# Loads of the second block in another order, and x's adding transfer moved to the seventh unit

## The chip, the cores and the metric

The kernel runs on one core of one Trainium2 chip. The metric is the device time of one launch in microseconds (us), the median of three runs. Profiles are of one execution each.

## What is computed

A decayed scan (an attention of the state-space kind, in chunks) is followed by a gated feed-forward layer. The reference, cut to what matters:

```python
def _attn_ref(x, a, B, C):                      # x: 4 x 8 x 768 x 32, B and C: 4 x 8 x 768 x 16
    log_a = np.log(np.clip(a, 1e-06, 1.0))
    for c in range(nc):                          # chunks of 32 steps
        cum = np.cumsum(la, axis=-1)
        L = np.exp(cum[:, :, :, None] - cum[:, :, None, :]) * causal
        M = np.einsum('bhin,bhjn->bhij', Cc, Bc) * L
        y_intra = np.einsum('bhij,bhjd->bhid', M, xc)
        y_inter = np.einsum('bhin,bhnd->bhid', Cc, state) * np.exp(cum)[:, :, :, None]
        y[:, :, sl] = y_intra + y_inter
        state = decay_full[:, :, None, None] * state + np.sum(Bx, axis=2)

def _moe_ref(x, w_gate, w_val, w_out):           # x: 3072 x 256, d_ff 1536
    g = x @ w_gate
    silu = g * (1.0 / (1.0 + np.exp(-g)))
    return (silu * (x @ w_val)) @ w_out
```

## The kernel before

**Tiling.** The 768 steps are cut into six blocks of 128 steps (k = 0 to 5; the text calls k = 1 the second block), each of two pieces of 64. One block holds 512 tokens (4 batches by 128 steps). Per block the scan part makes decays (`L` between steps, `E` for the carried state), scores `S`, the mixed matrix in `L`, states `T` and the output `y`; then the feed-forward part runs over 12 units of 128 hidden columns: `gate_val` (two PSUM banks, the tiles `gv`), `silu` on ACT, `product` on DVE (both write `sg`), a split of the product into a high and a low part (`hh`), and `project` into `po`.

**Two kinds of feed-forward matmul.** For the first block the first nine units (`WHOLE = 9`) multiply plain 32-bit floats: the weights `wg0w` to `wg8w` and x in `xf`. All others multiply high and low parts: weights `wg..h` and `wg..l`, x in `xh` and `xl`. So the first block's units 9, 10 and 11 are the first that read its `xh` and `xl`.

**Where the parts come from.** Each weight piece arrives as 64-bit integers' words (`wg9r`, loaded by `w_fetch`) and is turned into floats by a chain over engines: `w_magnitude` and `w_rest` on ACT, `w_range` on POOL for most pieces, `w_shift`, `w_sign` and `w_round` on DVE; then `w_high` on ACT. The low part of the first nine pieces is made by ACT writing the negative of the weight (`w_minus`) and POOL issuing a transfer that adds the weight to it (`w_low`, `accum_op=ALU.add`). x of the first block goes the same way: `first_high` and `first_minus` on ACT, twice each, and `first_low`, one adding transfer of 512 KB issued by POOL:

```python
    def first_low():
        ge.dma_start(xl[0], whole[0], accum_op=ALU.add)
```

Weight pieces 9 to 11 need no transfer: DVE subtracts (`w_low`).

**The second block's loads** are `bc` (B and C, 512 KB), `L` (the decays, each row sent to 64 partitions, two transfers of 520 KB), `xb` (x and B, 768 KB) and `E` (260 KB), all on SP's queue, which also issues the weight pieces. `heads_apart` (`Cz`) reads `bc`, `scan_j` reads `L`, `weigh_b` reads `xb`, `scan_n` reads `E`, all on DVE here.

**What sets the order.** Every step is an `Op` with an engine, a cost, a rank, what it needs and a `lag` that stands for the transfer behind an issue. `Plan.order` plays these through and issues the steps in the order that it finds; `plan.follow` adds needs "issued after" for the lists in `ORDER`. Each engine then runs its instructions in that order. A step with `lag` occupies a modelled bus, so a changed lag can move steps on every engine. All engine instructions have line 191, that of the recording helper; the tile names tell them apart.

Of the kernel before, what the change touches and what calls it, by code (L numbers as in the profile page):

```python
# [19 lines left out]
P = 128  # L20
# [24 lines left out]
class Plan:  # L45
# [19 lines left out]
    def add(self, engine, cost, run, rank, needs=(), takes=(), uses=(), gives=None, kind=None, lag=0.0, rows=1.0, slack=0.0):  # L65
        engines = [(engine, cost)] if cost is not None else engine
        self.ops.append(Op(engines, run, rank, needs, takes, uses, gives, kind, lag, rows, slack, cost is None))
# [134 lines left out]
def scan_moe_kernel(ctx: ExitStack, tc, aj, an, bc, xb, wgv, wo, cst, own, out):  # L202
    nc = tc.nc
    PSUM = bass.MemoryType.PSUM
    te, ve, se, ge, sp = (
        Ordered(tc, e) for e in (nc.tensor, nc.vector, nc.scalar, nc.gpsimd, nc.sync)
    )

    def pool(name, bufs, stack=ctx, **kw):
        return stack.enter_context(tc.tile_pool(name=name, bufs=bufs, **kw))  # L210
# [5 lines left out]
    raw = pool("raw", RAW)  # L216
# [14 lines left out]
    clipped = dram.tile([2, P, NA * W], F32, name="clipped")  # L231
# [79 lines left out]
    def first(b, i):  # L311
        return b < BATCH and not i
# [189 lines left out]
    xh, xl = {}, {}  # L502
# [170 lines left out]
    rest = {}  # L673
# [29 lines left out]
    def do(f, *a):  # L703
        return lambda *e: f(*a, *e)
# [6 lines left out]
    add = plan.add  # L711
# [10 lines left out]
    def due(k, f=0):  # L722

        return begin[k] + f * (GV if k else PACE0)

    def at(n):

        return divmod(n, NF)

    def due_sum(k, f):  # L730
        return begin_sum[k] + f * PO
# [12 lines left out]
    for i in range(NW):  # L744
        r = due(0, i) - 1.0 if i < NF else due_sum(0, 2 * (i - NF)) - 1.0
        if i < NF:
            add("SP", 0.48, do(w_fetch, i), r - 9.0, takes=[("raw", ("raw", i))], gives=("raw", i), lag=1.3)
        else:
            add("Act", 0.1, do(w_fetch, i, se), due(*at(LAST[i - NF])) + 2, [("si", *at(LAST[i - NF]))], takes=[("raw", ("raw", i))], gives=("raw", i), lag=1.3)
        add("Act", 0.57, do(w_magnitude, i, "Act"), r - 5.5, [("raw", i)], takes=[("sg" if i < NF else "w", ("w", i))], gives=("mag", i))  # L750
        far = i in FAR
        e, c = ("Pool", 2.2) if far else ("DVE", 0.335)
        add(e, c, do(w_range, i, ge if far else ve), r - 4.5, [("mag", i), *([("round", i - 1)] if i == 1 else [])], gives=("range", i))
        add("Act", 0.57, do(w_rest, i, "Act"), r - 4.5, [("raw", i), *([("xf", 3)] if i == 3 else [])], gives=("rest", i))
        add("DVE", 0.335, do(w_shift, i), r - 4.2, [("range", i)], gives=("shift", i))
        add("DVE", 0.6, do(w_sign, i), r - 3.9, [("shift", i)], gives=("sign", i))
        add("DVE", 0.6, do(w_round, i), r - 3.3, [("sign", i), ("rest", i)], uses=[("raw", i)], gives=("round", i))
        if i < WHOLE:
            r = due(1, i) - LATER
        add("Act", 0.57, do(w_high, i, "Act"), r - 2.7, [("round", i), ("gv", 0, 0, 0)], gives=("wh", i))  # L760
        whole_done = [("gv", 0, i, m) for m in range(2)]
        if i < WHOLE:
            add("Act", 0.57, do(w_minus, i), r - 2.6, [("round", i), ("gv", *at(MINUS[i]), 0)], gives=("minus", i))
            add("Pool", 1.2, do(w_low, i), r - 2.5, [("wh", i), ("minus", i), *whole_done], uses=[("w", i)], gives=("wl", i), lag=3.0)
        else:
            add("DVE", 0.6, do(w_low, i), r - 1.5, [("wh", i)], uses=[("w", i)], gives=("wl", i))


    add("-", 0.0, lambda: None, -7.9, gives="all", lag=0.9)
    add("Pool", 1.0, clip_all, -9, ["all"], gives="clipped")  # L770
    add("SP", 0.48, do(write_all, sp, slice(0, FEW)), -9, ["clipped"], gives="few", lag=1.5)
    add("Act", 0.1, do(write_all, se, slice(FEW, P)), -1.6, ["clipped", ("rest", 0)], gives="written", lag=1.5)


    for k in range(NB):
        r = due(k)
        SLACK = min(k / 2, 1.0)
        z = -5 if not k else r + LEAD[min(k, 3)]
        L, E, BC, XB, CZ, TT = ("L", k), ("E", k), ("bc", k), ("xb", k), ("Cz", k), ("T", k)
        add("-", 0.0, do(new_decays, k) if k else lambda: None, z - 12, [("decays", k - 1)] if k else [], takes=[("L", L), ("E", E)], gives=("decays", k))  # L780
        late = [("raw", LATE[k])] if k in LATE else []
# [12 lines left out]
        if not k:  # L794
            add("-", 0.0, lambda: None, -9, takes=[("xl", "rows")], gives="rows", lag=0.2)
            for i in range(3):
                add("DVE", 0.35, do(clip_rows, i), (-9, -8.9, -5)[i], ["rows", *([("scan0", 1)] if i == 2 else [])], gives=("clip", i))
            for b in range(BATCH + 1):
                r = z + 0.5 + b if b < BATCH else -1.3
                for i in range(2 if b < BATCH else 1):  # L800
                    t = ("spread", b, i)
                    add("PE", 0.25 if first(b, i) else 0.45, do(spread, b, i), r + 0.5 * i, [("clip", b % 2 if b < BATCH else 2), "pick"], takes=[("mm" if first(b, i) else "at", t)], uses=[t, "rows"], gives=t, kind="s")
                    need = [t, ("decays", 0)] + ([("scan0", b)] if i else [])
                    done = ("E", 0) if b == BATCH else ("L", 0, b) if i else ("scan0", b)
                    add("DVE", 0.63, do(scan_spread, b, i), r + 0.5 * i, need, uses=[t], gives=done)
        else:
            add("SP", 0.96, do(load_aj, k), FETCH["aj"] if k == 1 else z - 12, ["few", "written", ("decays", k), *late], gives=("aj", k), lag=4.3)
            add("SP", 0.48, do(load_an, k), FETCH["an"] if k == 1 else z - 9, ["few", "written", ("decays", k), *late], gives=("an", k), lag=2.4)
            for b in range(BATCH):
                add("DVE", 1.14, do(scan_j, k, b), z + 0.5 + b, [("aj", k)], gives=("L", k, b), slack=1.0)  # L810
            add("DVE", 1.17, do(scan_n, k), z + 6, [("an", k)], gives=("E", k), slack=1.0)
# [26 lines left out]
        uses = [L, E, XB, BC, *y, TT]  # L838
# [16 lines left out]
        if not k:  # L855
            add("-", 0.0, new_whole, -9, [("clip", 2)], takes=[("xl", "xf")], gives="xf")
            add("-", 0.0, do(new_x, 0), due(0, WHOLE) - 9, [("xf", i) for i in range(2 * K)], takes=[("xh", ("xh", 0)), ("xl", ("xl", 0))], gives=("x", 0))
            for g in range(2):
                r = due(0, WHOLE) - 7 + 2 * g
                add("Act", 0.57, do(first_high, g, "Act"), r, [("x", 0)], gives=("xh", 0, g))  # L860
                add("Act", 0.57, do(first_minus, g), r + 0.5, [("x", 0)], gives=("minus", "x", g))
            add("Pool", 1.2, first_low, due(0, WHOLE) - 4.5, [("minus", "x", g) for g in range(2)], uses=["xf"], gives=("xl", 0, 0), lag=3.0)
            for i in range(2 * K):
                add([("Act", 0.36)], None, do(x_whole, i), -1 + i / 10, [("vals", i) if i < 2 else ("y", 0), "xf"], uses=[y[i]], gives=("xf", i))
            continue
# [6 lines left out]
    for k in range(NB):  # L872
        xs = [(t, k, i) for t in ("xh", "xl") for i in range(2 * K if k else 2) if k or t == "xh" or not i]
        for f in range(NF):
            r = due(k, f)
            need = [*xs, ("wh", f), ("wl", f)]
            c = 1.4
            x = [("xh", k), ("xl", k)]
            if not k and f < WHOLE:
                need = [("round", f), *(("xf", i) for i in range(2 * K))]  # L880
                c = 1.72
                x = ["xf"]
            gv = [("gv", k, f, m) for m in range(2)]
# [5 lines left out]
            r = due_sum(k, f) - 4  # L889
# [4 lines left out]
        for n, (m, t, fs) in enumerate(sums_of(k)):  # L894
# [4 lines left out]
            r = due_sum(k, fs[0]) + n * 0.01  # L899
# [25 lines left out]
FETCH = dict(aj=10.0, an=35.0, bc=12.0, xb=31.0)  # L925
LATER = 3.0
WHOLE = 9
LAST = (5, 6, 9, 10, 11, 12)
MINUS = (3, 3, 4, 5, 9, 9, 10, 10, 11)
FEW = 8  # L930
# [1 line left out]
PAGE = 4.4  # L932
ORDER = (
    ["few", ("raw", 2)],
    [("raw", 8), ("bc", 1), ("aj", 1), ("raw", 9), ("xb", 1), ("raw", 10), ("an", 1), ("raw", 11)],
    [("xf", 3), ("mag", 2), ("rest", 2), ("mag", 3)],
    [("y", 0), ("xf", 2)],
)
LEAD = {1: -30.0, 2: -44.0, 3: -44.0}
LATE = {}  # L940
# [49 lines left out]
```

## Time and profile before

| | |
|---|---|
| median of 3 runs | 353.0 us |
| the runs | 351.2, 353.0, 353.35 us |
| the profiled execution's own time | 353.25 us |
| its span, first to last instruction | 351.4 us |
| instructions | 7415 |
| TensorE clock granted, mean | 0.998 |
| bytes moved by DMA | 30.98 MB, mean 88 GB/s |

The profiled execution's own time is 1.85 us above its span. The page gives each engine's busy time and then the span in 40 slices of 8.8 us; the views behind it (the timeline of one engine, the chain that ended last, sums over windows, the list of DMA issues) are in microseconds from the span's start. A bracket in a timeline row tells how long the engine was idle ahead of it and what ended that.

### The profile page before, as it was taken

The page shows a single profiled execution, that of the slowest core. Times are in us where ns is not written, and L with a number is a line of the kernel's source. Part 1 is how long each engine was busy: PE and PEld are TensorE (multiplying, and loading weights), DVE is VectorE, ACT ScalarE, POOL GpSimd, SP SyncE. Part 2 cuts the span into 40 slices and gives each one's busy share as a digit, 9 for nine tenths or more (in the row PEclk, how much of TensorE's full clock was granted, in tenths as well). Part 3 has the DMA queues.
Part 4 walks back from the last instruction along what each step waited for, and adds up shares of the span by engine and source line. Part 5 has one row for each costly group of instructions (what it writes and reads, how often), then busy time and mean ns, then how long its engine had stood idle before and what let it go on. Part 6 is the DMA issues. An engine that isn't in the chain of part 4 may idle for free.

```text
span 351.4 us, 7415 instructions
## 1 busy us (share of the span) xinstructions
PE 341.9 (97%) x3195; PEld 267.2 (76%) x3196; DVE 232.1 (66%) x418; ACT 121.8 (35%) x222; POOL 45.3 (13%) x36
## 2 busy tenths in 40 slices
PE   7999988999999999999999999999999999999996
PEld 5644436888878888888888888888888888888895
DVE  6996999999888856676447677447666440465220
ACT  3785766643445422212322222231212230222221
POOL 2395563522012000000000000000000000000000
PEclk9999999999999999999999999999999999999999
DMA  7999972994000671000382000281100000100001
GB/s 262 289 316 246 259 162 69 247 249 130 0 2 2 185 179 60 0 2 3 105 184 76 0 2 2 74 211 39 41 3 2 2 2 0 60 2 0 0 2 60
DMA packets 9935, 30.98 MB, mean 88 GB/s; under 512 B 1287, under 2 KB 2055, under 8 KB 9263
## 3 DMA queue, kind: packets, MB, share of 16 engines
q1 hardware_dynamic: 7168, 24.23, 23.6%
q0 software_dynamic: 1440, 2.88, 4.7%
q10 hardware_dynamic: 1295, 3.40, 3.2%
q8 instruction: 25, 0.41, 0.5%
q14 instruction: 7, 0.06, 0.1%
HBM read 24.28 MB, written 3.35 MB: 79 GB/s over the span
## 4 chain that ended last, share of the span: by engine, by line
PE 83%; DMA 6%; DVE 5%; issue 1%; ACT 1%; ACTq 0%; DVEq 0%; SPq 0%
PE gv L191 49%; PE po L191 28%; DMA wg10r<-in_wgv 6%; PE y L191 4%; PE S L191 1%; DVE wg8w L191 1%; DVE sg L191 1%; DVE wg2w L191 1%; DVE wg9w L191 0%; DVE wg1w L191 0%; DVE wg0w L191 0%; DVE L L191 0%; DVE E L191 0%; DVE wg10w L191 0%; DVE T L191 0%
## 5 line engine op out<-in xcount | busy, mean ns | idle before, releaser
L191 DVE TENSOR_TENSOR sg<-gv,sg 128x512 f32<-128x512 f32 x72 | 49.5, 687 | 65.4 <-PE gv L191 65.2
L191 ACT ACTIVATE sg<-gv 128x512 f32<-128x512 f32 x72 | 43.0, 597 | 105.5 <-PE gv L191 105.5
L191 DVE TENSOR_TENSOR hh<-sg,hh 128x512 fp32r<-128x512 f32 x72 | 49.3, 690 | 12.5 <-ACT hh L191 11.0
L191 ACT CAST hh<-sg 128x512 fp32r<-128x512 f32 x34 | 21.2, 623 | 30.1 <-PE po L191 17.7
L191 DVE TENSOR_TENSOR_SCAN L<-L,dj 128x520 f32<-128x520 f32 x20 | 24.6, 1248 | 10.2 <-DMA L<-clipped 10.2
L191 ACT COPY ob<-po 128x512 f32<-128x512 f32 (+1 forms) x13 | 7.2, 555 | 48.7 <-PE po L191 48.2
L191 DVE CAST hh<-sg 128x512 fp32r<-128x512 f32 x38 | 16.5, 434 | 2.4 <-PE po L191 1.2
L191 PE MATMUL po<-hh,wo0h 128*128 128x512 f32 (+1 forms) x52 | 15.3, 377 | 0.0
L191 PE MATMUL po<-hh,wo3h 128*128 128x512 f32 (+1 forms) x52 | 15.2, 375 | 0.0
L191 PE MATMUL po<-hh,wo1h 128*128 128x512 f32 (+1 forms) x52 | 15.2, 375 | 0.0
L191 PE MATMUL po<-hh,wo4h 128*128 128x512 f32 (+1 forms) x52 | 15.1, 373 | 0.0
L191 DVE TENSOR_TENSOR L<-S,L 128x512 f32<-128x512 f32 x24 | 15.1, 681 | 0.0
L191 PE MATMUL po<-hh,wo5h 128*128 128x512 f32 (+1 forms) x52 | 15.1, 373 | 0.0
L191 PE MATMUL po<-hh,wo2h 128*128 128x512 f32 (+1 forms) x52 | 15.0, 373 | 0.0
L191 PE MATMUL y<-L,xb 64*32 64x64 f32 x768 | 11.5, 239 | 0.0
L191 PEld LDWEIGHTS po<-hh,wo0h 128*128 128x128 f32 x52 | 9.5, 188 | 2.2 <-DVE hh L191 0.3
L191 PEld LDWEIGHTS y<-L,xb 64*32 64x32 f32 x768 | 9.5, 112 | 2.0 <-issue 1.8
L191 PEld LDWEIGHTS po<-hh,wo4h 128*128 128x128 f32 x52 | 9.5, 188 | 1.7
L191 PEld LDWEIGHTS po<-hh,wo5h 128*128 128x128 f32 x52 | 9.5, 188 | 1.7
L191 PEld LDWEIGHTS po<-hh,wo2h 128*128 128x128 f32 x52 | 9.5, 188 | 1.7
L191 PEld LDWEIGHTS po<-hh,wo1h 128*128 128x128 f32 x52 | 9.4, 188 | 1.8
L191 PEld LDWEIGHTS po<-hh,wo3h 128*128 128x128 f32 x52 | 9.4, 188 | 1.7
(298 smaller groups left out, 754.0 us busy)
## 6 DMA issues: line engine op xcount, KB each, us to landing
L<-clipped SPq DMA_DIRECT2D x10, 520.0 KB, 17.0
xb<-in_xb SPq DMA_DIRECT2D x6, 768.0 KB, 10.5
bc<-in_bc SPq DMA_DIRECT2D x6, 512.0 KB
out<-ob SPq DMA_DIRECT2D x11, 256.0 KB, 2.0
E<-clipped SPq DMA_DIRECT2D x5, 260.0 KB
wg0r<-in_wgv SPq DMA_DIRECT2D x1, 512.0 KB
wg1r<-in_wgv SPq DMA_DIRECT2D x1, 512.0 KB
wg2r<-in_wgv SPq DMA_DIRECT2D x1, 512.0 KB
```

What stands on the lines that cost most here:

```text
L191: ins = getattr(self.engine, name)(*a, **k)
```

## The change

Two kinds of lines change. The first are four `lag` values of the plan and the lists of `ORDER`: the second block's loads go `bc`, `aj` (which loads `L`), `xb`, `an` (which loads `E`) as before, but each of the last three now follows one weight piece more; a new list says that `Cz` of the second block is issued after `round` of piece 6. The second is one need: `first_minus` now waits for ("gv", 0, 6, 0), the first gate matmul of the seventh unit, so that the negative of x is written later, and with it the adding transfer `first_low` comes later.

```diff
-            add("Pool", 1.2, do(w_low, i), r - 2.5, [...], uses=[("w", i)], gives=("wl", i), lag=3.0)
+            add("Pool", 1.2, do(w_low, i), r - 2.5, [...], uses=[("w", i)], gives=("wl", i), lag=1.6)
...
-    add("SP", 0.48, do(write_all, sp, slice(0, FEW)), -9, ["clipped"], gives="few", lag=1.5)
-    add("Act", 0.1, do(write_all, se, slice(FEW, P)), -1.6, ["clipped", ("rest", 0)], gives="written", lag=1.5)
+    add("SP", 0.48, do(write_all, sp, slice(0, FEW)), -9, ["clipped"], gives="few", lag=2.6)
+    add("Act", 0.1, do(write_all, se, slice(FEW, P)), -1.6, ["clipped", ("rest", 0)], gives="written", lag=0.3)
...
-            add("SP", 0.96, do(load_aj, k), ..., gives=("aj", k), lag=4.3)
-            add("SP", 0.48, do(load_an, k), ..., gives=("an", k), lag=2.4)
+            add("SP", 0.96, do(load_aj, k), ..., gives=("aj", k), lag=4.8)
+            add("SP", 0.48, do(load_an, k), ..., gives=("an", k), lag=1.8)
...
-                add("Act", 0.57, do(first_minus, g), r + 0.5, [("x", 0)], gives=("minus", "x", g))
-            add("Pool", 1.2, first_low, ..., uses=["xf"], gives=("xl", 0, 0), lag=3.0)
+                add("Act", 0.57, do(first_minus, g), r + 0.5, [("x", 0), ("gv", 0, 6, 0)], gives=("minus", "x", g))
+            add("Pool", 1.2, first_low, ..., uses=["xf"], gives=("xl", 0, 0), lag=1.6)
...
-    [("raw", 8), ("bc", 1), ("aj", 1), ("raw", 9), ("xb", 1), ("raw", 10), ("an", 1), ("raw", 11)],
+    [("raw", 8), ("bc", 1), ("raw", 9), ("aj", 1), ("raw", 10), ("xb", 1), ("raw", 11), ("an", 1)],
...
+    [("round", 6), ("Cz", 1)],
```

Up to the issue of `wg8r` SP's row is the same, and so are POOL's and ACT's up to the eighth range and the third silu. SP's row from there (`in_wgv` is the weights' input; minus is before, plus is now):

```order
 L191 DMA wg8r<-in_wgv 128x1024
-L191 DMA bc_424<-in_bc 128x1024
+L191 DMA bc_421<-in_bc 128x1024
+L191 DMA wg9r<-in_wgv 128x1024
 L191 DMA L_372<-clipped 64x2080 x2
-L191 DMA wg9r<-in_wgv 128x1024
-L191 DMA xb_443<-in_xb 128x1536
 L191 DMA wg10r<-in_wgv 128x1024
+L191 DMA xb_446<-in_xb 128x1536
+L191 DMA wg11r<-in_wgv 128x1024
 L191 DMA E_373<-clipped 128x1x520
-L191 DMA wg11r<-in_wgv 128x1024
```

Weight pieces 9, 10 and 11 each moved ahead of one load of the second block: `L`, `xb` and `E`.

DVE's row after the range of piece 5 came in, before (a TENSOR_SCALAR on `wg..w` is a shift, a SCALAR_TENSOR_TENSOR on `wg..w` a sign, an ISA a rounding, a TENSOR_TENSOR on `sg` a product, a SCALAR_TENSOR_TENSOR on `L` a scan):

```order
L191 TENSOR_SCALAR wg5w<-wg5w 128x512
L191 TENSOR_SCALAR Cz_463<-bc_424,cs 128x4x128 x2
L191 SCALAR_TENSOR_TENSOR wg5w<-wg5r,wg5w 128x512
L191 TENSOR_TENSOR sg_2_461<-gv_2_1_457,sg_2_461 128x512
L191 ISA wg5w<-wg5r,wg5w 128x1024
L191 TENSOR_SCALAR wg6w<-wg6w 128x512
L191 SCALAR_TENSOR_TENSOR wg6w<-wg6r,wg6w 128x512
L191 TENSOR_SCALAR wg7w<-wg7w 128x512
L191 ISA wg6w<-wg6r,wg6w 128x1024
L191 SCALAR_TENSOR_TENSOR wg7w<-wg7r,wg7w 128x512
L191 TENSOR_TENSOR sg_3_484<-gv_3_1_480,sg_3_484 128x512
L191 SCALAR_TENSOR_TENSOR L_372<-L_372,dj 128x520 x2
```

And the same place of DVE's row now:

```order
L191 TENSOR_SCALAR wg5w<-wg5w 128x512
L191 SCALAR_TENSOR_TENSOR wg5w<-wg5r,wg5w 128x512
L191 ISA wg5w<-wg5r,wg5w 128x1024
L191 TENSOR_TENSOR sg_2_461<-gv_2_1_457,sg_2_461 128x512
L191 TENSOR_SCALAR wg6w<-wg6w 128x512
L191 SCALAR_TENSOR_TENSOR wg6w<-wg6r,wg6w 128x512
L191 ISA wg6w<-wg6r,wg6w 128x1024
L191 TENSOR_SCALAR Cz_488<-bc_421,cs 128x4x128 x2
L191 TENSOR_TENSOR sg_3_482<-gv_3_1_479,sg_3_482 128x512
L191 TENSOR_SCALAR wg7w<-wg7w 128x512
L191 SCALAR_TENSOR_TENSOR wg7w<-wg7r,wg7w 128x512
L191 TENSOR_SCALAR wg8w<-wg8w 128x512
```

`Cz`, which waits for `bc`, went behind six steps of weight work; the scans of `L` follow right behind the last row shown. Further on in DVE's row, the sign of piece 11 stood ahead of the rounding of piece 10 and now stands behind it, and the low part of output piece 0 (`wo0l`) went behind the four steps that make the second block's `xl`.

POOL's row, now, from the range of piece 8 on (a TENSOR_SCALAR is a range, a DMA an adding transfer):

```order
L191 TENSOR_SCALAR wg8w<-wg8w 128x512
L191 TENSOR_SCALAR wg9w<-wg9w 128x512
L191 DMA wg0l<-wg0w 128x512
L191 TENSOR_SCALAR wg10w<-wg10w 128x512
L191 DMA wg1l<-wg1w 128x512
L191 TENSOR_SCALAR wg11w<-wg11w 128x512
L191 DMA wg2l<-wg2w 128x512
L191 DMA wg3l<-wg3w 128x512
L191 TENSOR_SCALAR wo0w<-wo0w 128x512
L191 DMA xl_386<-xf 128x1024
```

The transfer into `xl` stood between the first two of these rows and is now behind them all; the rest kept its order, but for `wg8l`, which went ahead of the range of `wo1w`. On ACT the two writes of `xl` went from ahead of the fourth silu to behind the seventh, and the magnitude of output piece 0 (`wo0w`, which waits for `wo0r`) went ahead of the seventh silu. PE's row is the same up to the second block's ninth unit: there units 8 and 9 (counted from 0) change places.

More of the change, by code (lines that the diff above doesn't have):

```diff
@@ L763, in scan_moe_kernel @@
             add("Act", 0.57, do(w_minus, i), r - 2.6, [("round", i), ("gv", *at(MINUS[i]), 0)], gives=("minus", i))
-            add("Pool", 1.2, do(w_low, i), r - 2.5, [("wh", i), ("minus", i), *whole_done], uses=[("w", i)], gives=("wl", i), lag=3.0)
+            add("Pool", 1.2, do(w_low, i), r - 2.5, [("wh", i), ("minus", i), *whole_done], uses=[("w", i)], gives=("wl", i), lag=1.6)
         else:
@@ L806, in scan_moe_kernel @@
         else:
-            add("SP", 0.96, do(load_aj, k), FETCH["aj"] if k == 1 else z - 12, ["few", "written", ("decays", k), *late], gives=("aj", k), lag=4.3)
-            add("SP", 0.48, do(load_an, k), FETCH["an"] if k == 1 else z - 9, ["few", "written", ("decays", k), *late], gives=("an", k), lag=2.4)
+            add("SP", 0.96, do(load_aj, k), FETCH["aj"] if k == 1 else z - 12, ["few", "written", ("decays", k), *late], gives=("aj", k), lag=4.8)
+            add("SP", 0.48, do(load_an, k), FETCH["an"] if k == 1 else z - 9, ["few", "written", ("decays", k), *late], gives=("an", k), lag=1.8)
             for b in range(BATCH):
@@ L860, in scan_moe_kernel @@
                 add("Act", 0.57, do(first_high, g, "Act"), r, [("x", 0)], gives=("xh", 0, g))
-                add("Act", 0.57, do(first_minus, g), r + 0.5, [("x", 0)], gives=("minus", "x", g))
-            add("Pool", 1.2, first_low, due(0, WHOLE) - 4.5, [("minus", "x", g) for g in range(2)], uses=["xf"], gives=("xl", 0, 0), lag=3.0)
+                add("Act", 0.57, do(first_minus, g), r + 0.5, [("x", 0), ("gv", 0, 6, 0)], gives=("minus", "x", g))
+            add("Pool", 1.2, first_low, due(0, WHOLE) - 4.5, [("minus", "x", g) for g in range(2)], uses=["xf"], gives=("xl", 0, 0), lag=1.6)
             for i in range(2 * K):
```

## The prediction

> **What bounds the kernel now.** I read the page first, then the chain of work that ended last, then the timelines of PE, DVE, ACT and POOL over the stretch that the chain points at, and last the queues.
>
> ```profile
> span 351.4 us, 7415 instructions
> PE   7999988999999999999999999999999999999996
> DVE  6996999999888856676447677447666440465220
> DMA  7999972994000671000382000281100000100001
> ```
>
> PE is busy in all but a few slices, and those lie ahead of slice 7, that is ahead of 62 us. DVE is full over the same slices, and so are the DMA engines up to slice 5 (44 us). From there on only PE is full.
>
> ```profile
> 21.58 19.67 DMA wg10r<-in_wgv
> ...
> 57.39 0.63 ACT wg10h L191
> ...
> 58.06 3.04 PE gv L191 x12
> ...
> 62.97 35.69 PE gv L191 x156
> ```
>
> The chain says the same: from 58.06 to the end it runs through PE almost alone; ahead of it, it goes through the load of weight piece 10 and then mostly through DVE to the rounding of that piece. So the end moves by as much as PE's eleventh unit, now at 58.06, moves, as long as PE stays without gaps behind it. PE's own gaps up to there:
>
> ```profile
> 43.05 3.70 PE L191 MATMUL gv<-xf,wg7w 128*128 128x512 f32 x8 [0.72 <-ACT sg L191]
> 48.16 3.67 PE L191 MATMUL gv<-xf,wg8w 128*128 128x512 f32 x8 [1.42 <-DVE wg8w L191]
> ...
> 54.56 0.63 PE L191 MATMUL gv<-xl,wg9h 128*128 128x512 f32 x2 [0.47 <-issue]
> 55.03 0.61 PE L191 MATMUL gv<-xh,wg9l 128*128 128x512 f32 x2
> ...
> 58.06 0.73 PE L191 MATMUL gv<-xh,wg10h 128*128 128x512 f32 x2 [1.06 <-ACT wg10h L191]
> ```
>
> They sum to 0.72 + 1.42 + 0.47 + 1.06 = 3.7 us, and three of the four wait for a weight that DVE or ACT had not finished. What made DVE late shows in its own timeline:
>
> ```profile
> 26.16 0.42 DVE L191 TENSOR_SCALAR wg5w<-wg5w 128x512 int32<-128x512 int32 x1
> 29.29 1.23 DVE L191 TENSOR_SCALAR Cz<-bc,cs 128x512 f32<-128x512 f32 x2 [2.70 <-DMA bc<-in_bc]
> ...
> 31.04 0.68 DVE L191 TENSOR_TENSOR sg<-gv,sg 128x512 f32<-128x512 f32 x1
> 31.64 0.68 DVE L191 CUSTOM_DVE_ANT_0 wg5w<-wg5r,wg5w 128x1024 uint16<-128x1024 uint16 x1
> ...
> 35.43 2.73 DVE L191 TENSOR_TENSOR_SCAN L<-L,dj 128x520 f32<-128x520 f32 x2
> 38.57 0.29 DVE L191 TENSOR_TENSOR xb<-xb,L 128x128 f32<-128x128 f32 x1 [0.41 <-DMA xb<-in_xb]
> ...
> 43.03 0.69 DVE L191 TENSOR_TENSOR sg<-gv,sg 128x512 f32<-128x512 f32 x1 [0.28 <-ACT sg L191]
> ...
> 45.32 1.50 DVE L191 SCALAR_TENSOR_TENSOR wg8w<-wg8r,wg8w 128x512 int32<-128x512 int32 x1
> ...
> 56.68 0.68 DVE L191 CUSTOM_DVE_ANT_0 wg10w<-wg10r,wg10w 128x1024 uint16<-128x1024 uint16 x1
> ```
>
> Three brackets (2.70, 0.41, 0.28) are DVE's only idle time between 26 us and the rounding of piece 10 at 56.68. A step of 128x512 follows the next by 31.64 - 31.04 = 0.60.
>
> **The change, part by part.** The sum is made at the start of unit 10 on PE (58.06), against the profiled execution's own 353.25 us (0.25 above the median of 353.0).
>
> *The wait for bc.* `Cz` now stands behind five steps of 0.60 and a shift (0.42) that it stood ahead of: 3.4 us of work where DVE sat 2.70. DVE reaches it at about 29.9, after bc's landing of before (29.29). So the 2.70 go, even if bc comes no sooner.
>
> *The loads' order.*
>
> ```profile
> 16.19 0.37 SPq L191 DMA_DIRECT2D bc<-in_bc  x1
> 16.61 1.98 SPq L191 DMA_DIRECT2D L<-clipped  x2
> 18.69 0.52 SPq L191 DMA_DIRECT2D wg9r<-in_wgv  x1
> ...
> DMA to landing us min/median/max: 17.0/17.0/17.0
> ...
> 15.00:20.00 5.00, 4.95 (x34) 2.32 (x28) 4.91 (x12) 4.41 (x9) 1.95 (x2) 1.00 1.02 411
> ...
> 25.00:30.00 5.00, 5.00 (x13) 2.23 (x12) 2.26 (x5) 4.42 (x9) 5.00 (x3) 1.00 1.01 181
> ```
>
> The one figure "to landing" is that of tile L: 17.0 us, so L landed at 33.6 at the earliest, and at 35.43 at the latest, where the scans began without waiting. The windows' last number is GB/s at a full DMA share: 411 while weights stream, 181 while L is among them. Now the scans stand right behind a shift, and DVE is there at 35.43 - 2.70 + 0.42 = 33.1 (the shift of piece 8 is what came ahead of them). Wg9r is put ahead of L: 512 KB at 411 GB/s are 1.3 us. But it was carried at the slow rate within L's time before, and bc with it, which is now out of that stretch; and bc's tail no longer competes. Bounds for the new wait on L: 0 (L in by 33.1) and 2.3 (35.43 as the latest of before). I take 0.8, between, nearer to 33.6 as the row that measures a landing.
>
> *xb and the silu.* The other two waits (0.41 on xb, 0.28 behind ACT) hang on xb and on wg10r, for which ACT stood still:
>
> ```profile
> 41.28 0.68 ACT L191 ACTIVATE wg10w<-wg10r 128x512 f32<-128x512 f32 x1 [2.30 <-DMA wg10r<-in_wgv]
> 41.37 0.36 ACTq L191 DMA_DIRECT2D wo0r<-in_wo  x1
> ```
>
> wg10r goes ahead of xb, and xl's transfer no longer shares the engines with either, so both waits go: 0.69. Bounds 0 and 0.69. wo0r is issued from behind wg10w's place on ACT's queue; its magnitude now stands ahead of the seventh silu, and unit 8 needs the bank that this silu frees, at about 48.16 - 3 = 45. Issued no later than 41.37 it has 3.6 us; I cost it at nothing, under cover of unit 7's 3.7 us on PE; if wo0r is later than that, unit 8 is late next.
>
> *DVE's order.* One step (the sign of piece 11) leaves the stretch ahead of piece 10's rounding: 0.60. The low part of wo0 moves behind the second block's xl; it lies behind 58.06 beside PE's work and is costed at nothing.
>
> *xl's adding transfer* is the cost side. Rows of POOL and of the list of DMA issues (last number: us to landing):
>
> ```profile
> 30.19 1.03 POOL L191 DMA_DIRECT2D xl<-xf  x1
> ...
> 45.31 2.25 POOL L191 TENSOR_SCALAR wg11w<-wg11w 128x512 f32<-128x512 f32 x1
> 47.18 1.29 POOL L191 DMA_DIRECT2D wg2l<-wg2w  x1
> 47.78 1.60 POOL L191 DMA_DIRECT2D wg3l<-wg3w  x1
> 52.73 1.95 POOL L191 TENSOR_SCALAR wo0w<-wo0w 128x512 f32<-128x512 f32 x1 [3.35 <-ACT wo0w L191]
> ...
> xl<-xf POOLq DMA_DIRECT2D x1, 512.0 KB, 10.9
> ...
> wg1l<-wg1w POOLq DMA_DIRECT2D x1, 256.0 KB, 3.6
> ```
>
> Before, it was issued at 30.19 and in at 41.1, 13 us ahead of its first reader at 54.56. Now it is queued behind piece 11's range, wg2l, wg3l and wo0's range. From the start of that range to wg3l's end are 49.38 - 45.31 = 4.1 us, and 1.95 more for wo0's range: 6.0. The range of piece 11 hangs on wg10r and wg11r; those were held up by xl and xb, and I put it 4 to 6 us earlier than 45.31, at 39.3 to 41.3. That issues xl at 45.3 to 47.3. Its time to landing is bounded by 3.6 (wg1l, half its size, on idle engines) and 10.9 (itself among the loads); by 45 us the second block's loads are in, so I take 3.6 plus half of it again, 5.4: landing at 50.7 to 52.7. Needed: unit 10 is to start at 58.06 - 3.2 = 54.9, and from xl's first use to the end of unit 9 there are four pairs, 4 x (55.03 - 54.56) = 1.9, so it must be there by 53.0. Cost taken: nothing, with 0.3 to 2.3 us to spare. At the upper bound it is late by 3.2 to 5.2.
>
> The Trainium skill's "DMA: Bandwidth & Descriptors", section "Anatomy of one DMA — SWDGE (gpsimd) path", gives such a transfer about 2.0 us plus its bytes at 436 GB/s; as an estimate by that page xl would take 3.2 us and land 2.2 us sooner than I take, with the sum the same. The trace differs: for 256 KB that fit gives 2.6 where wg1l took 3.6, and the measured row decides.
>
> ACT's two writes of xl move from ahead of the fourth silu to behind the seventh. ACT had idle time at both places; cost nothing, since the silu and the casts that PE needs stand ahead of them.
>
> *Sum:* 2.70 + 0.69 + 0.60 - 0.80 = 3.2 us gained at unit 10. Behind it PE has no gap before, and DVE's and ACT's work shifts with it. 353.25 - 3.2 = 350.05, say 350.0.
>
> **The rivals.**
>
> *More is gained (348.3 to 349.2).* L lands by 33.1, so nothing is given back: 2.70 + 0.69 + 0.60 = 4.0, 349.25; and where a DVE step is not drawn out beside POOL, as the sign of piece 8 was (1.50 for 0.68 of its like), 0.8 more. For it: bc and wg9r leave the slow stretch. Against it: 33.6 as the earliest landing seen, and POOL has as much to do as before.
>
> *One wait for another (351.5 to 353.3).* L comes as late as 35.43 or later, since wg9r is ahead of it: the wait for bc comes back as a wait for L. That gives back 2.3 us, a gain of 1.7 (351.55); if xb, E or wo0r come no sooner either, the rest goes too and the change does nothing: 353.25. For it: the same bytes go over the same full engines.
>
> *xl comes late (353.5 to 355.2), slower.* One place: PE's third matmul of unit 9. With 10.9 us from issue, xl lands at 56.2 to 58.2; unit 10 then starts 1.9 later, at 58.1 to 60.1, against 58.06: up to 2.0 lost, 355.25. It decides from a landing at 56.2 on; a loss of over 1% would need one past 59.7. For it: POOL issues it in DVE's fullest stretch, where wg3l's issue took 1.60 us. Against: DMA share. In the window of the loads it was 1.0; behind them it is not.
>
> ```profile
> 41.00:48.00 7.00, 1.00 0.83 235
> ```
>
> The Trainium skill's "SBUF — State Buffer", section "SBUF: two separate sides", speaks for this rival: while DVE runs certain modes, POOL cannot write a transfer's descriptors, and the engines sit waiting for them. No row here separates that from POOL's own time.
>
> **How the numbers follow.** The case of the sum (349.3 to 351.5) has 0.55, more gained 0.18, one wait for another 0.16, xl late 0.09, and 0.02 is left. The predicted time is that of the sum, 350.0. The range from 348.3 to 353.3 takes in the first three, and leaves out xl late and some of the tails. About 1% (3.5 us) is what a measurement of this kernel can tell from no change: faster means under 349.5, slower over 356.5. Under 349.5 lie the whole of "more gained" and a quarter of the sum's case (0.18 + 0.14 = 0.32). Over 356.5 lies only an xl past 59.7 with what is left, 0.05. The rest, 0.63, is within 1%.
>
> **What would show it.** Right: no DVE wait ahead of `Cz`, a short one at most ahead of the scans of L at about 33 to 34, unit 8 on PE at 45 without waiting for wg8w, unit 10 at about 54.9, PE without gaps from there, xl landed by 53. Wrong: a wait of PE for xl in unit 9; a DVE wait of 2 us or more for L or xb; ACT standing at wo0w while unit 8 waits for the seventh silu; or a gap on PE behind unit 11, where the second block's xh and xl have little to spare.

## The result and the profile after

| | before | after |
|---|---|---|
| median | 352.03 us (14 runs) | 354.18 us (14 runs) |
| lowest to highest | 349.72 to 354.1 us | 351.31 to 355.67 us |
| the profiled execution, its span | 353.25 us, 351.4 us | 355.67 us, 353.6 us |

The ratio after to before is 1.0056, 95% interval 1.0031 to 1.0081: in this comparison the change makes the kernel slower by about 2 us. Run twice more beside the experiments it gave 1.0027 (0.9998 to 1.0055) and 1.0048 (1.0018 to 1.0078). 350.0 us and a gain had been forecast. Disturbed executions, with a lower clock and over 1.5% above the kernel's fastest, are left out of every ratio, among them 4 of the 12 of order_only, below, whose profile is of one of the four, so only its waits are read.

The page of the changed kernel, the span and the slices:

```profile
span 353.6 us, 7407 instructions
PE   7999979998999999999999999999999999999996
DVE  6989899778799874677448677548567440465220
PEclk9999999999999999999999999999999999999999
```

A slice is 8.8 us. Before, PE's digits below 9 stood in the sixth and seventh slices and in the first and last; now there is one in the tenth (80 to 88 us), behind the stretch that the prediction worked on. What stands there shows in the chain of work that ended last (start, duration, what):

```profile
62.95 4.10 PE gv L191 x18
67.05 0.27 SPq L191
67.31 0.04 issue
67.36 17.39 DMA xb<-in_xb
...
84.84 0.70 DVE xb L191 x3
85.54 1.15 DVE L L191
86.69 1.13 DVE E L191
87.82 0.59 DVE sg L191
```

Before, the chain ran through PE alone from 62.97 on. Now it leaves PE for a load: the third block's `xb`, then three groups of DVE work on the third block's loads, and a product. PE's timeline of the changed kernel at that place, and at unit 10 of the first block:

```profile
58.19 0.61 PE L191 MATMUL gv<-xh,wg10h 128*128 128x512 f32 x2
...
79.33 0.62 PE L191 MATMUL gv<-xh,wg5h 128*128 128x512 f32 x2
...
86.09 0.61 PE L191 MATMUL gv<-xl,wg7h 128*128 128x512 f32 x2
88.46 0.72 PE L191 MATMUL gv<-xh,wg7h 128*128 128x512 f32 x2 [1.75 <-DVE sg L191]
...
89.95 0.62 PE L191 MATMUL gv<-xh,wg8h 128*128 128x512 f32 x2
```

PE's timeline of the kernel before has no wait there:

```profile
79.47 0.61 PE L191 MATMUL gv<-xh,wg5h 128*128 128x512 f32 x2
...
87.63 0.61 PE L191 MATMUL gv<-xh,wg9h 128*128 128x512 f32 x2
```

Unit 10 starts at 58.19, with no wait ahead of it (58.06 and a wait of 1.06 before). The second half of the second block's unit 7 then waits 1.75 us for a product of DVE that frees its bank. DVE's timeline of the changed kernel shows what held that product up:

```profile
75.91 0.69 DVE L191 TENSOR_TENSOR hh<-sg,hh 128x512 fp32r<-128x512 f32 x1
78.95 1.24 DVE L191 TENSOR_TENSOR_SCAN L<-L,dj 128x520 f32<-128x520 f32 x1 [2.35 <-DMA L<-clipped]
80.11 0.67 DVE L191 TENSOR_TENSOR sg<-gv,sg 128x512 f32<-128x512 f32 x1
...
82.97 0.66 DVE L191 TENSOR_TENSOR sg<-gv,sg 128x512 f32<-128x512 f32 x1
84.84 0.70 DVE L191 TENSOR_TENSOR xb<-xb,L 128x128 f32<-128x128 f32 x3 [1.21 <-DMA xb<-in_xb]
...
87.74 0.67 DVE L191 TENSOR_TENSOR sg<-gv,sg 128x512 f32<-128x512 f32 x1
```

And the same steps in the kernel before:

```profile
79.76 0.68 DVE L191 TENSOR_TENSOR sg<-gv,sg 128x512 f32<-128x512 f32 x1
...
81.79 1.23 DVE L191 TENSOR_TENSOR_SCAN L<-L,dj 128x520 f32<-128x520 f32 x1
82.94 0.67 DVE L191 TENSOR_TENSOR sg<-gv,sg 128x512 f32<-128x512 f32 x1
...
86.38 0.69 DVE L191 TENSOR_TENSOR xb<-xb,L 128x128 f32<-128x128 f32 x3
```

Before, product 4 (79.76) stands ahead of the first scan of the third block's `L` (81.79), and neither the scan nor the weighing of `xb` waits. Now the first scan stands ahead of product 3 (80.11), and the weighing of `xb` ahead of product 5 (87.74, at 82.94 before). The loads are hardly sooner: SP issues the third block's `bc` at 63.04 (63.06 before), `L` at 63.53 (63.55) and `xb` at 67.36 (68.75). So two products that were ready stood in DVE's row behind 2.35 + 1.21 us of waiting for loads; ACT's silu for product 3, for one, had ended at 76.05. From 79.33 to the start of the ninth unit (89.95) PE needs 10.62 us; before it needed 8.16 (79.47 to 87.63). These 2.46 us are more than the whole difference of the spans (2.2).

### The profile page after: what moved, and what is told of

Read it like the earlier page. It is cut to its first block, busy times and chain, and to the rows that moved or that the text cites. A ratio compares the mean times of both kernels' runs of the same rounds, so it can differ in the third digit from the quotient of the medians.

```text
span 353.6 us, 7407 instructions
## 1 busy us (share of the span) xinstructions
PE 342.9 (97%) x3196; PEld 268.4 (76%) x3196; DVE 232.0 (66%) x416; ACT 123.0 (35%) x224; POOL 45.2 (13%) x36
## 4 chain that ended last, share of the span: by engine, by line
PE 78%; DMA 16%; DVE 4%; issue 1%; ACT 1%; SPq 0%; DVEq 0%; ACTq 0%
PE gv L191 44%; PE po L191 28%; DMA E<-clipped 5%; DMA xb<-in_xb 5%; PE y L191 4%; DMA wg8r<-in_wgv 3%; DMA wg1r<-in_wgv 2%; PE S L191 1%; DVE L L191 1%; DVE E L191 1%; DMA rows<-in_aj 1%; DVE sg L191 1%; DVE wg8w L191 0%; DVE wg9w L191 0%; SPq L191 0%
```

## The experiments

Each kernel was timed in about 12 executions (xl_late_alone in 6), beside the kernel before on the same chip; the table also has two distances between starts of units on PE in its profiled execution, and how many of the executions that its ratio uses had a mean clock under 0.997. "First block" is from unit 1 to unit 11; "second block" is from unit 4 to the start of the ninth unit, 10.88 us where PE never stands.

| kernel | ratio to before (95%) | first block, us | second block, us | low clock |
|---|---|---|---|---|
| before, on record | 1 | 43.34 | 10.88 | 3 of 132 |
| null | 0.9982 (0.9955 to 1.0009) | 41.13 | 10.88 | 0 of 12 |
| changed, on record | 1.0056 (1.0031 to 1.0081) | 41.46 | 13.34 | 7 of 14 |
| again | 1.0027 (0.9998 to 1.0055) | 40.28 | 12.44 | 1 of 12 |
| changed_3 | 1.0048 (1.0018 to 1.0078) | 40.88 | 13.00 | 5 of 11 |
| scans_behind_pr4 | 0.9992 (0.9960 to 1.0025) | 41.98 | 10.88 | 3 of 12 |
| scans_as_before | 1.0007 (0.9977 to 1.0037) | 43.16 | 10.88 | 2 of 12 |
| early_scans | 1.0053 (1.0025 to 1.0080) | 42.91 | 11.00 | 0 of 12 |
| early_scans_2 | 1.0030 (0.9997 to 1.0064) | 42.10 | 11.92 | 1 of 12 |
| lag_only | 1.0033 (1.0003 to 1.0063) | 42.26 | 11.79 | 0 of 11 |
| order_only | 1.0010 (0.9978 to 1.0042) | 45.93 | 10.87 | 3 of 8 |
| cz_later | 1.0011 (0.9984 to 1.0039) | 42.44 | 10.88 | 3 of 12 |
| cz_and_e | 1.0009 (0.9979 to 1.0040) | 42.45 | 10.88 | 0 of 12 |
| order_and_e | 0.9997 (0.9968 to 1.0025) | 40.68 | 10.88 | 0 of 12 |
| e_hold_alone | 1.0042 (1.0012 to 1.0071) | 41.75 | 12.66 | 0 of 12 |
| e_behind_round8 | 0.9962 (0.9928 to 0.9996) | 40.18 | 10.88 | 1 of 12 |
| both_holds_again | 0.9989 (0.9959 to 1.0019) | 42.02 | 10.91 | 1 of 12 |
| xl_late_alone | 1.0385 (1.0342 to 1.0429) | 44.11 | 10.88 | 6 of 6 |

The theory was that the early scans of the third block make the loss. The first rival: the changed kernel's first units. In its profile on record the write of the clipped decays stood 2 us later than before, unit 1 of PE started at 21.42 (19.56), and these instructions are the same in both kernels. The second rival: the loads' new order brings nothing.

**The changed kernel again, and the scans held.** `again` is the change as it is. In scans_behind_pr4 it gets more lists in `ORDER`, which hold the third block's scans and weighings:

```diff
+    *([("pr", 1, 4), ("L", 2, b)] for b in range(BATCH)), [("pr", 1, 6), ("E", 2)],
+    *([("pr", 1, 6), ("bt", 2, b)] for b in range(BATCH)),
```

> The changed kernel once more, for a second profile of it. Theory (wait in the second block): DVE again stands about 2.4 us ahead of the third block's first scan of L and about 1.2 us ahead of the weighing of xb, PE waits about 1.75 us for product 5, ratio 1.003 to 1.008; the start is not part of it, so the clipped decays are written at about 9.8 us this time, unit 1 of PE starts at about 19.6 instead of 21.4, and unit 10 at about 56.3. Rival (the start): the write stands at about 12.0 again and unit 1 at about 21.4.

> The change, with the third block's scans of L held behind product 4 of the second block and its weighings of xb and scan of E behind product 6. Theory: no DVE wait for L or xb there, no PE wait for product 5, about 2.4 us less than the changed kernel, 351.8, ratio to before 0.993 to 0.998 (the 1.9 us of unit 10 stay). Rival, the start: nothing changes, ratio 1.003 to 1.008. Rival, the loads' order brings nothing by itself: the stall goes, and the ratio is 0.999 to 1.001.

In scans_as_before the lists write the row nearly as it was before the change:

```diff
+    *([("pr", 1, 4 if b < 1 else 5), ("L", 2, b)] for b in range(3)),
+    [("pr", 1, 6), ("bt", 2, 0), ("L", 2, 3), ("E", 2)], *([("pr", 1, 6), ("bt", 2, b)] for b in range(1, BATCH)),
```

> The change, with DVE's row of the second block from product 4 to product 7 written nearly as it was before (scan, wo2l, product 5, two scans, product 6, three weighings of xb, scan, scan of E, product 7). Theory: as with the other version that holds the scans, 351.5 to 352.2, ratio 0.993 to 0.998. Rival, the start: 1.003 to 1.008.

The start is not the loss: unit 1 of `again` started at 19.91, and the stall in its second block was there all the same (12.44 - 10.88 = 1.56 us). With the scans held it is gone in both versions, and so is the loss. But the times are those of before, not below, as the second rival had it: the gain at unit 10 did not show in them. One cause of that stands in the profile of scans_as_before. PE's timeline:

```profile
48.24 5.37 PE L191 MATMUL gv<-xf,wg8w 128*128 128x512 f32 x8 [2.48 <-DVE wg8w L191]
```

and the windows of the same kernel (times, busy us of PE, PEld, DVE, ACT and POOL, then the granted clock, the DMA share and GB/s):

```profile
44.00:48.00 4.00, 1.76 (x5) 0.45 (x3) 4.00 (x5) 2.20 (x5) 4.00 (x4) 1.00 0.89 216
48.00:52.00 4.00, 3.76 (x5) 1.65 (x6) 4.00 (x8) 2.71 (x5) 1.12 (x2) 0.57 0.91 169
```

PE stood 2.48 us for `wg8w`, and the unit behind it ran at a clock of 0.57 in that window: 5.37 us for eight matmuls that take 3.67 at full clock (the row of `wg8w` in the prediction), 1.70 us lost on top of the wait. In the changed kernel's own profile the wait for `wg8w` was 1.88 us and the clock stayed at 1.00; so of these two waits only the longer one had this price. The Trainium skill's "TensorE: Matmul & The Clock Gate", section "HAM oscillation — how this bites in real kernels", warns of idle gaps of PE over about 3.4 us. Here 2.48 were enough.

The length of a single wait does not settle it. PE's timeline of xl_late_alone, a kernel described below, and two windows of it:

```profile
53.76 0.63 PE L191 MATMUL gv<-xl,wg9h 128*128 128x512 f32 x2 [1.89 <-issue]
...
56.13 1.28 PE L191 MATMUL y<-L,xb 64*32 64x64 f32 x64 [1.27 <-DVE T L191]
...
68.60 0.72 PE L191 MATMUL gv<-xh,wg11h 128*128 128x512 f32 x2 [3.18 <-DVE sg L191]
```

```profile
57.00:59.00 2.00, 2.00 (x88) 1.83 (x74) 2.00 (x9) 0.00 (x0) 0.00 (x0) 0.50 0.00 0
69.00:70.00 1.00, 1.00 (x6) 0.69 (x4) 0.47 (x1) 0.00 (x0) 0.00 (x0) 1.00 0.97 172
```

Behind waits of 1.89 and 1.27 us close together the clock was 0.50, and behind one of 3.18 us it was 1.00. What decides is not shown here.

**The early scans alone.** The kernel before gets one list, which puts the scans and weighings where the changed kernel has them:

```diff
+    [("pr", 1, 2), ("L", 2, 0), ("pr", 1, 3), ("L", 2, 1), ("L", 2, 2), ("pr", 1, 4),
+     ("bt", 2, 0), ("bt", 2, 1), ("bt", 2, 2), ("pr", 1, 5), ("pr", 1, 6)],
```

> The kernel before, with only the third block's scans put ahead of products 3 and 4 and three weighings of xb ahead of product 5, as they stand in the changed kernel; its loads keep their order. Theory: the scans wait a little for L (under 1 us, since wo2's steps still stand ahead), the weighing of xb waits until 84.5, product 5 comes at about 87.5 instead of 82.9 and PE waits 1.5 to 2.5 us for it: 1.5 to 2.5 us slower than before, ratio 1.004 to 1.007. Rivals (the start, or the loads' order): no difference to before, 0.999 to 1.001.

> The early scans in the kernel before once more, since the first profile showed a wait of 1.72 us for xb on DVE but product 5 just in time for PE, and yet the timed executions were 2.0 us slower in the mean. Theory: the wait is at a threshold, and this profile shows PE waiting 0.5 to 2 us for product 5 at unit 7, ratio 1.003 to 1.007. Rival: the loss is elsewhere, and product 5 is in time again with the ratio as before.

Slower, by 0.53% and 0.30%. The first profile had the wait of DVE for `xb` (1.72 us), but PE lost only 11.00 - 10.88 = 0.12 us; the second lost 1.04. So PE's loss varies from one execution to the next, and the first batch's loss in the mean of the spans (352.0 against 350.0 us) is larger than either profile shows; that part isn't explained.

**One kind of line alone.** lag_only has the `lag` values of the change (six of them, as the diff shows, not four) and nothing else, order_only the two lists of `ORDER` and nothing else; null is the kernel before.

> The kernel before, unchanged, for a second profile of it beside the others. The span of its profile on record (351.4) is above the mean of its 35 timed executions (350.0). Theory: its first units are what varies from one execution to the next, so a second profile differs from the first ahead of unit 11 of PE by some us, and by less than 0.5 us behind it; ratio 0.998 to 1.002. Rival: the second block varies too, and a wait of DVE for L or xb shows there in this profile.

> The kernel before with the planner's new lags alone: no load and no transfer of the first block is told to move. In DVE's row the third block's scan of L stands ahead of product 3 and three weighings of xb ahead of product 5, as in the changed kernel. Theory: the wait for xb comes, 1.0 to 1.2 us, and PE waits 1 to 2 us at unit 7 of the second block; 1 to 2.2 us slower than before, ratio 1.003 to 1.006. Rival (the first units or the loads are the loss): 0.999 to 1.001.

> The kernel before with the two lists alone (the loads' order, and Cz behind the rounding of piece 6); xl's transfer stays where it was. The third block's scans stand behind product 4 and wo2l here. Theory (the loss is the early scans): no wait for L or xb in the second block, and a part of the 1.9 us of unit 10, ratio 0.994 to 0.999. Rival (the loads' order brings nothing by itself): 0.999 to 1.001 with unit 10 at the same distance from unit 1 as before (38.5 us).

lag_only is slower by 0.33%, although it moves no load of the first block. DVE in it:

```profile
77.24 1.24 DVE L191 TENSOR_TENSOR_SCAN L<-L,dj 128x520 f32<-128x520 f32 x1 [1.86 <-DMA L<-clipped]
...
83.49 0.69 DVE L191 TENSOR_TENSOR xb<-xb,L 128x128 f32<-128x128 f32 x3 [1.57 <-DMA xb<-in_xb]
```

So the early scans come from the lags, not from the lists. Among the lags it is the one of POOL's adding transfers for the weights (`w_low`, 3.0 to 1.6) that moves them in the plan: put into the kernel before by itself it brings the scans ahead of product 3, and each of the other lags by itself leaves them behind product 4 (this is the order that the plan finds; no chip run was made of it).

order_only has no early scans and gains nothing either. DVE in it:

```profile
46.51 1.24 DVE L191 TENSOR_TENSOR_SCAN E<-E,dn 128x520 f32<-128x520 f32 x1 [2.48 <-DMA E<-clipped]
47.66 0.67 DVE L191 SCALAR_TENSOR_TENSOR wg8w<-wg8r,wg8w 128x512 int32<-128x512 int32 x1
```

The scan of `E` stands ahead of piece 8's sign, `E` is now the last load of the list, and PE's unit 8 waits 5.11 us for that piece.

null gave the number that the prediction lacked. DVE's wait for `bc` in it:

```profile
27.11 0.88 DVE L191 TENSOR_SCALAR Cz<-bc,cs 128x512 f32<-128x512 f32 x2 [0.55 <-DMA bc<-in_bc]
```

The same row in early_scans, whose first block is the same as before's:

```profile
27.98 1.42 DVE L191 TENSOR_SCALAR Cz<-bc,cs 128x512 f32<-128x512 f32 x2 [1.39 <-DMA bc<-in_bc]
```

And in early_scans_2:

```profile
28.74 1.26 DVE L191 TENSOR_SCALAR Cz<-bc,cs 128x512 f32<-128x512 f32 x2 [1.76 <-DMA bc<-in_bc]
```

0.55, 1.39 and 1.76 us, where the profile on record had 2.70; lag_only, whose loads stand as before too, had 2.47. The first block's distance on PE goes along with it only roughly (41.13, 42.91, 42.10 and 43.34 us). The execution on record was among the longer ones of its kernel: its span is 351.4 us, and the mean of the 35 executions of that kernel in the first batch of experiments is 350.0.

**The waits of the first block.** cz_later is the kernel before with the one list `[("round", 6), ("Cz", 1)]`; cz_and_e has `[("round", 8), ("E", 1)]` as well. e_behind_round8 is scans_behind_pr4 with that second list.

> The kernel before with Cz alone bound behind the rounding of piece 6; the loads and xl stay. Theory (the wait for bc was 0.55 to 2.70 in the profiles of that order, 1.8 in the mean, and the distance from unit 1 to unit 11 of PE follows it from 41.1 to 43.3 us): DVE has no wait for bc, part of it comes back as a wait for L, the distance is 41.0 to 42.0, mean span 349.0 to 349.8, ratio 0.995 to 1.000. Prediction on record (2.70 us gained at the least by this step, 0.8 given back): ratio 0.994 or less.

> The kernel before with Cz behind the rounding of piece 6 and the first block's scan of E behind the rounding of piece 8; the loads and xl stay. Theory: no wait for bc, no wait for E ahead of piece 8, unit 8 of PE waits 0 to 0.7 us; ratio 0.993 to 0.998, the best of this batch. Rival: the scan of E is missed by the carried sums in unit 9, and PE stands there 0.5 us or more; ratio 0.999 to 1.002.

> The change with two holds: the third block's scans and weighings as in scans_behind_pr4, and in the first block the scan of E put behind the rounding of piece 8 (in the changed kernel it stands ahead of that piece's sign, and waited 0.69 us for E there; with the loads' order alone 2.48). Theory (E holds up wg8w): unit 8 of PE waits 1.2 us less for wg8w than in the changed kernel's profiles (0.79 to 1.88), so 0 to 0.7; no execution falls to a clock of 0.995; the mean span is 349.3 or less, ratio 0.993 to 0.999. Rival (wg8w is late because of L and xb, not of E): unit 8 still waits 1 us or more, ratio 0.999 to 1.003.

Taking the wait for `bc` away gains nothing by itself. DVE in cz_later:

```profile
32.88 2.37 DVE L191 TENSOR_TENSOR_SCAN L<-L,dj 128x520 f32<-128x520 f32 x2 [0.77 <-DMA L<-clipped]
36.34 0.29 DVE L191 TENSOR_TENSOR xb<-xb,L 128x128 f32<-128x128 f32 x1 [0.40 <-DMA xb<-in_xb]
```

PE in the same kernel:

```profile
46.56 3.67 PE L191 MATMUL gv<-xf,wg8w 128*128 128x512 f32 x8 [1.21 <-DVE wg8w L191]
```

It comes back as waits for `L` and `xb`, and unit 8 still waits 1.21 us for `wg8w`. With `E` held too (cz_and_e) none of 12 executions has the low clock, where 3 of 12 had it, but the time is no shorter. In e_behind_round8 PE's unit 8 waits only 0.15 us, for a product:

```profile
45.15 1.88 PE L191 MATMUL gv<-xf,wg8w 128*128 128x512 f32 x4
47.19 1.98 PE L191 MATMUL gv<-xf,wg8w 128*128 128x512 f32 x4 [0.15 <-DVE sg L191]
```

Its ratio of 0.9962 is the lowest of all.

**x's transfer alone.** The kernel before with the new need of `first_minus` and the lists of scans_behind_pr4:

```diff
-    add("Act", 0.57, do(first_minus, g), r + 0.5, [("x", 0)], ...)
+    add("Act", 0.57, do(first_minus, g), r + 0.5, [("x", 0), ("gv", 0, 6, 0)], ...)
```

> The kernel before with xl's adding transfer alone bound to unit 6 of PE (the seventh), the loads in their old order, and the third block's scans held behind product 4 and its weighings behind product 6. Theory (the transfer itself costs nothing): PE does not wait for xl in unit 9, ratio 0.998 to 1.002. Rival (the late transfer costs): PE waits 0.5 us or more for xl in unit 9 or DVE's steps beside it stretch (the rounding of piece 8 took 1.08 us, the weighing of bc 1.36), ratio 1.002 to 1.005. The time outside the span is 2.0 us if the late transfer brings it, and 1.8 if not.

13 us slower, and not by the transfer. ACT in it:

```profile
74.57 0.65 ACT L191 ACTIVATE wo2r<-wo2r 128x512 int32<-128x512 uint32 x1 [7.30 <-DMA wo2r<-in_wo]
```

In this kernel the plan puts a step of output piece 2, whose load had only just been asked for (62.14), ahead of a silu; DVE waits 6.26 us for that silu and PE 5.50 for it. So this kernel does not price the transfer. It shows that one new need can move steps far behind it.

**Two terms apart, and the best version again.** e_hold_alone is the change with `[("round", 8), ("E", 1)]` only; order_and_e is order_only with that list; the other two are repeats on the same chip.

> The changed kernel a third time, on the same chip as the three beside it. Both terms (scans in the second block, scan of E in the first) are in it. Theory: ratio 1.002 to 1.008; some of its 12 executions fall to a clock of 0.993 to 0.995; PE waits for product 5 in the second block.

> The changed kernel with the scan of E put behind the rounding of piece 8, and the third block's scans left where the change has them, ahead of product 3. Theory of two terms, each by itself: the first block is as in e_behind_round8 (40.2 us from unit 1 to unit 11 of PE, no clock under 0.997), the second loses 1.5 to 2.5 us at products 3 and 5, so 1.5 to 2.5 us over the version with both holds: ratio 0.999 to 1.003. Rival (the scan of E was the whole loss): as the version with both holds, ratio 0.994 to 0.998. Rival (the scans were the whole): as the changed kernel, 1.003 to 1.008.

> The kernel before with the two lists (loads' order, and Cz behind the rounding of piece 6) and the scan of E behind the rounding of piece 8; xl early, as before. Theory: with the loads' order alone 7 of 12 executions fell to a clock of 0.99 behind a wait for E; without that wait none does, unit 8 of PE waits under 0.7 us, ratio 0.994 to 0.999. Rival (the gain of the version with both holds comes from xl's move): ratio 0.999 to 1.003.

> The change with both holds once more, beside the changed kernel on the same chip: ratio to before 0.993 to 0.999 again, 1.5 to 3 us under the changed kernel. Rival (the first result was the chip's scatter): 0.999 or more.

e_hold_alone is as slow as the change (1.0042): the early scans are the loss. Its expectation of two terms that add did not come out: the stall in the second block is 1.78 us, as expected, but the first block took 41.75 us where 40.2 were expected, so the hold of `E` brought no gain that can be seen. With the scans held as well, on the same chip, the median falls from 353.24 to 351.74 us. order_and_e has one of the shortest first blocks (40.68) without moving x's transfer, and is as fast as before (0.9997); so what the version with both holds owes to the transfer's move, if anything, is open. The version with both holds beats the changed kernel side by side (351.74 against 353.32 us); against before it was 0.9962 once and 0.9989 with an interval over 1 the other time, so a gain over before is not certain.

All kernels of the table but xl_late_alone fall into two groups. The seven timings with early scans have ratios of 1.0027 to 1.0056 and a stall in the second block of 0.12 to 2.46 us; the nine others have 0.9962 to 1.0011 and at most 0.03 us. The kernel before against itself (null) gave 0.9982, so a difference of 0.2% within a group says little.

changed_3 shows one more wait. PE in it:

```profile
51.82 0.49 PE L191 MATMUL gv<-xl,wg9h 128*128 128x512 f32 x1 [0.64 <-DMA xl<-xf]
...
79.41 0.73 PE L191 MATMUL gv<-xh,wg5h 128*128 128x512 f32 x2 [0.94 <-DVE sg L191]
...
85.74 0.73 PE L191 MATMUL gv<-xh,wg7h 128*128 128x512 f32 x2 [0.46 <-DVE sg L191]
```

In this execution the front was early, and x's transfer, issued at 46.61, came 0.64 us late.

## Why the prediction was wrong, point by point

- **The step that failed** is "Behind it PE has no gap before, and DVE's and ACT's work shifts with it." It does not shift with it: the plan builds one row for DVE over all blocks, and the changed lags put the third block's scans ahead of product 3 in the second block. That cost 2.46, 1.56 and 2.12 us in three profiles of the changed kernel. Shown by lag_only and the early scans (the loss without the loads' order) and by the two versions that hold the scans (the change without the loss). The new row could be read before any run; the prediction, and the rows of DVE shown ahead of it, stop at the first block, where its sum was made.
- **The wait for bc, 2.70.** That it goes was right: in all three profiles of the changed kernel `Cz` runs without a wait. Its size was a draw: 0.55 to 2.70 in four profiles of the same instructions. The 353.25 us that the sum starts from are of the execution with the largest of them, 1.2 us above the median of the 14. And cz_later shows that a wait of DVE for one load turns into waits for the next ones.
- **The new wait for L, 0.80.** Measured 0.68 in the profile on record; none in the other two.

```profile
32.10 1.22 DVE L191 TENSOR_SCALAR Cz<-bc,cs 128x512 f32<-128x512 f32 x2
...
36.02 2.38 DVE L191 TENSOR_TENSOR_SCAN L<-L,dj 128x520 f32<-128x520 f32 x2 [0.68 <-DMA L<-clipped]
39.50 0.49 DVE L191 TENSOR_TENSOR xb<-xb,L 128x128 f32<-128x128 f32 x2 [0.52 <-DMA xb<-in_xb]
44.37 1.24 DVE L191 TENSOR_TENSOR_SCAN E<-E,dn 128x520 f32<-128x520 f32 x1 [0.69 <-DMA E<-clipped]
```

- **The waits for xb and the silu, 0.69 to go.** The one for `xb` stayed (0.52 above), and one for `E` came (0.69), which had no term: the sum asked only what the loads that moved forward win, and `E`, put last, lost. It is a matter of the execution too: `xb` 0.34 and none in the other two profiles of the changed kernel, `E` none in both.
- **wg8w at 45 us without a wait.** Wrong: PE waited 1.88 us for it in the profile on record, 0.79 in `again` and not at all in changed_3. It also has a price that the prediction did not know: of the executions counted, 21 of 69 with the new loads' order and `E` ahead of piece 8 had a low clock, 2 of 60 where `E` was held, and 3 of 144 of the kernel before; cz_later, with the old order, had 3 of 12. A low clock right behind this wait is seen in the profile of scans_as_before; for the others only the counts speak.
- **xl's transfer at nothing.** Nearly right. It was issued at 48.40, 45.10 and 46.61 and took 5.8, 6.3 and 5.2 us (5.4 were taken). PE waited for it by name in one of three profiles, 0.64 us. A rival had this mechanism, with a larger price and a different reason for a slower kernel.
- **3.2 us gained at unit 10.** From unit 1 to unit 11 the means are 42.37 us (four profiles of the old first block, 41.13 to 43.34) and 40.87 us (three of the changed kernel, 40.28 to 41.46): 1.5 us. The two versions that hold only the third block's scans have the same instructions in the first block and took 41.98 and 43.16 us; with them, and without the 1.70 us of low clock in the second, the mean is 41.21 and the gain 1.2 us. That is under half of what was forecast, and the two sets of profiles overlap.
- **Three of PE's four gaps wait for a weight.** Two do (`wg8w` and `wg10h`); the row of unit 7 waits for ACT's silu, and the fourth names no releaser. The sum does not use the count.

Put together: 1.2 gained in the first block, 2.05 lost in the second (mean of the three), 0.16 gained behind it (40.47 against 40.63 us from its unit 11 to the third block's unit 0), 13 of 37 executions at 1.7 us for the low clock (0.6), and 0.23 us outside the span (below). That is a loss of 1.5 us; the three ratios say 1.0 to 2.0. The first two terms are means of a few profiles that differ by a microsecond and more, so the agreement is rough.

## What to carry to other kernels

Where a planner orders all engines, a changed cost or delay moves steps in stages that the diff does not touch: read every engine's new row to its end, and look for steps that need a load and now stand ahead of steps that free a bank. A wait seen in one execution is a sample; before it is taken as a term, look whether the profiled execution is a typical one, and ask which load the engine meets next. A load put to the end of a list needs its reader moved behind the work that others wait for; here that made low clocks rarer, but no gain in time by it alone was shown.

## What was not expected of the hardware

- A wait of PE of 2.48 us was followed by a window at 0.57 of the clock (1.70 us more for one unit), and one of 1.88 us was not; in xl_late_alone waits of 1.89 and 1.27 us close together were followed by a clock of 0.50, and one of 3.18 us by 1.00. No single length divides them.
- The time outside the span was 2.0 us in every kernel with the whole change (2.01 to 2.02 in the mean of each) and 1.8 us in every other (1.77 to 1.80). None of the parts alone brings it. What it is stays open.
- In unit 9 PE has a gap at its first uses of `xl` of up to 1.89 us for which the profile names no releaser, in kernels with x's transfer early (0.47 us before, 1.13 in null) and late (0.46 on record, 1.45 in e_hold_alone, 1.89 in xl_late_alone). It stays open too.
